# An adaLN transformer block on one core: the MLP's slices and output units in turn, in groups of four and two, with clamp, products and the second norm moved off VectorE

## The chip, the core and the metric

The kernel runs on one core of a Trainium2 chip. A core has five engines with queues of their own: TensorE (PE; its weight loads are listed as PEld), VectorE (DVE), ScalarE (ACT), GpSimd (POOL) and SyncE (SP), which issues all of this kernel's DMAs. Each engine runs its queue in order and waits on semaphores of the others. The metric is the device time of one execution in microseconds (us), as the median of several runs. Chances below speak of faster and slower by over 0.5%, which is about what a measurement of this kernel can tell from no change.

## The reference

```python
x = A_x                                        # 1 x 2048 x 512, fp32
mod = (silu(c) @ w_mod).reshape(1, 6, 1, 512)
sa, ca, ga, sb, cb, gb = (mod[:, i] for i in range(6))
h = layernorm(x) * (1 + ca) + sa
x = x + ga * attention(h, A_wqkv, A_wo)        # 32 heads of 16, softmax over all 2048 keys
h = layernorm(x) * (1 + cb) + sb
x = x + gb * (mish(h @ B_w1 + B_b1) @ B_w2)    # 512 -> 1792 -> 512, mish(h) = h * tanh(softplus(h))
```

With e = exp(h) and p = e(e + 2), tanh(softplus(h)) is p / (p + 2). The kernel caps the exponent's argument at HCAP = 10 and takes the reciprocal as exp(-ln(p + 2)), refined by one Newton step. Matrix products are made of three, from high and low parts of their factors (hi x hi, hi x lo, lo x hi).

## The kernel before

**Steps.** Attention is a loop of 512 steps (T). A step t handles, for one group of four heads and one block of 512 queries, one chunk of 128 keys: four score products (L507), four exponentials on ACT (L513) and the four products with the values for step t-2 (L531). It also makes four products for the row maxima of a group 20 steps (PRO) ahead (L470), which DVE reduces (L472), up to step 491. Sixteen steps finish a head group; eight groups (128 steps) finish a query block. The row maxima of a group are put together every 16 steps (L481 to L490).

**Slots.** Score and maximum products use 64 of the array's 128 rows, and two products in different halves run side by side. MLP and projection products are split into two halves of 64 rows (`mm_half`, L128), the first half of a unit's share in an even step, the second in the odd step after it. A *unit* is a list of matmuls that add up into one bank. `next_part` (L989) takes a unit of at most 8 matmuls whole into a pair of steps, and a longer one in two halves. Part of the maxima change over to the half that has fewer products (L1067). The six banks `ring` are shared by scores and maxima, `bk` with tags ms and acc is for units and values.

**Units beside attention.** For each of the first three query blocks (`block`, L746), once its attention is ready, 4 units project (`wo_unit`, 12 matmuls, L767), then 14 up slices (`up_unit`, 12 matmuls and the Mish, L808) and down units (`down_unit`, L825) for each group of slices and each 128 rows i. A unit is taken from a queue in order, once its ready time has come. Groups are of 5, 5 and 4 slices in blocks 0 and 1, so 15, 15 and 12 matmuls; in block 2 of 4, 4, 3 and 3, of which the last two (eight units) are held for the tail. The fourth block's projection and MLP are done in the tail, when attention has ended.

**Half steps.** `at(h, f)` runs f at half step h; a step t has half steps 2t and 2t+1 (at its middle). What a unit's end sets off is placed by h: for an up slice the bias at once, the clamp one half step later, then its exponential, the product p on DVE and h times p on POOL, the logarithm, and with the reciprocal's exponential all of POOL's rest (L719 to L735).

**Buffers.** Tags of the pool `mp` give a number of buffers: hb 3, ee 2, rr 2, a_h and a_l 7 each (NA), w2 7 (it also takes the projection's weights), w1 2; yd shares rr's two. A new use of a buffer waits for the last reader of the old one.

**Lines.** Second norm: `layernorm` (L100; statistics on DVE, L104 and L105, three POOL operations L106, L107, L109). Splits into high and low part: L95 and L98 on POOL. Attention's output is divided and split on POOL at L574, L95 and L98 after its denominators have gone to memory and back (L567, L569). Output units are copied by ACT (L835) and added on POOL (L836).

Of the kernel before, what the change touches and what calls it, by code (L numbers as in the profile page):

```python
# [18 lines left out]
def adaln_block(ctx: ExitStack, tc: tile.TileContext, x, wqkv, wo, w1, b1, w2, c, w_mod, out):  # L19
    nc = tc.nc  # L20
# [640 lines left out]
    def load_wo(k):  # L661
        return load_split("w2", NA, woscr[k])

# [3 lines left out]
    def load_w2(f):  # L667
        return load_split("w2", NA, w2scr[f])

    def w1v(w, v, k):  # L670
        return w[:, v, k * P:(k + 1) * P]

    def load_y(qb, i):
        y = mst["p"].tile([P, D], F32, tag=f"y{i}", name="y", bufs=1)
# [18 lines left out]
    def mish(f, acc, tail):  # L693

        mp = mst["p"]
        hb = mp.tile([P, TB], F32, tag="hb", name="hb", bufs=3)
        ee = mp.tile([P, TB], F32, tag="ee", name="ee", bufs=2)
        rr = mp.tile([P, TB], F32, tag="rr", name="rr", bufs=2)
        qq = mp.tile([P, TB], F32, tag="qq", name="qq", bufs=1)
        a_h = mp.tile([P, TB], F32R, tag="a_h", name="a_h", bufs=NA)  # L700
        a_l = mp.tile([P, TB], F32R, tag="a_l", name="a_l", bufs=NA)

        def s1(late=False):
            if late:
                nc.vector.tensor_scalar_add(hb, acc, b1c[:, f:f + 1])
            else:
                nc.scalar.activation(hb, acc, AF.Identity, bias=b1c[:, f:f + 1])

        def s2():
            nc.scalar.activation(ee, hb, AF.Relu, bias=hcap, scale=-1.0)  # L710

        def s2b():
            nc.scalar.activation(ee, ee, AF.Exp, bias=hcap, scale=-1.0)  # L713

        def s3():
            nc.vector.scalar_tensor_tensor(ee, ee, 2.0, ee, op0=ALU.add, op1=ALU.mult)  # L716
            (nc.vector if tail else nc.gpsimd).tensor_mul(hb, hb, ee)  # L717

        def s4():  # L719
            nc.scalar.activation(rr, ee, AF.Ln, bias=two)  # L720

        def s5():
            nc.scalar.activation(rr, rr, AF.Exp, scale=-1.0)  # L723
            if tail:
                nc.vector.scalar_tensor_tensor(qq, ee, 2.0, rr, op0=ALU.add, op1=ALU.mult)
                nc.vector.scalar_tensor_tensor(rr, qq, 2.0, rr, op0=ALU.subtract, op1=ALU.mult)
                nc.vector.scalar_tensor_tensor(hb, hb, -1.0, rr, op0=ALU.mult, op1=ALU.mult)
            else:
                nc.gpsimd.tensor_scalar(ee, ee, 1.0, 2.0, op0=ALU.mult, op1=ALU.add)
                nc.gpsimd.tensor_mul(qq, ee, rr)  # L730
                nc.gpsimd.tensor_scalar(qq, qq, -1.0, 2.0, op0=ALU.mult, op1=ALU.add)
                nc.gpsimd.tensor_mul(rr, rr, qq)  # L732
                nc.gpsimd.tensor_mul(hb, hb, rr)  # L733
            hi_copy("v" if tail and f > FT - 4 else "p", a_h, hb)
            lo_sub("v" if tail and f > FT - 4 else "p", a_l, hb, a_h)  # L735

        return (a_h, a_l), (s1, s2, s2b, s3, s4, s5)
# [5 lines left out]
    first_loads_of, early_loads_of = {}, {}  # L743
    NA = 7

    def block(qb, t0):  # L746

        xn, y, act, w1s, w2s, wos, done, hx = {}, {}, {}, {}, {}, {}, {}, []
        cuts = (0, 5, 10, 14) if qb < NB - 2 else (0, 4, 8, 11, 14)
        groups = [list(range(a, b)) for a, b in zip(cuts, cuts[1:])]  # L750
# [6 lines left out]
        def early_loads(h):  # L757
            load(h, wos, load_wo, range(DK - 1))

        def first_loads(h):  # L760
            load(h + 1, wos, load_wo, range(len(wos), DK))
            load(h + 2, y, lambda i: load_y(qb, i), range(4))
            load(h + 9, w1s, load_w1, range(2))
            load(h + 10, w2s, load_w2, range(NA - DK))
            done["w"] = h + 3

        def wo_unit(i, tag):  # L767
# [7 lines left out]
            def fin(h):  # L775
                nc.vector.tensor_add(y[i], acc, y[i])

                def norm():
                    xn[i], a = norm_y(y[i])
                    at(h + 3, a)  # L780
# [3 lines left out]
                if i == 3:  # L784
                    load(h + 1, w2s, load_w2, range(NA - DK, NA))
# [465 lines left out]
```

## Time and profile before

| what | us |
|---|---|
| median of three runs (1737.65 to 1745.74) | 1743.94 |
| the profiled execution | 1742.38 |
| its span on the core | 1740.6 |
| PE busy | 1699.3 |
| DVE busy | 1464.0 |
| ACT busy | 1341.4 |
| POOL busy | 752.8 |

The span is the time from the first to the last instruction on the core; a run's own time is some 2 us longer. A group's row reads: line, engine, operation, out <- in with shapes, count | busy time in all, mean of one in ns | idle time of the engine just before, and what ended it. A timeline's row reads: start, length, engine, line, operation, count, and in brackets the idle time before it and its releaser. A window's row gives for each engine the busy time and in brackets the number of instructions, then the granted clock and the share of the DMA engines. Busy time of PE counts overlapping matmuls once, and includes time in which one drains.

### The profile page before, as it was taken

The page shows a single profiled execution, that of the slowest core. Times are in us where ns is not written, and L with a number is a line of the kernel's source. Part 1 is how long each engine was busy: PE and PEld are TensorE (multiplying, and loading weights), DVE is VectorE, ACT ScalarE, POOL GpSimd, SP SyncE. Part 2 cuts the span into 40 slices and gives each one's busy share as a digit, 9 for nine tenths or more (in the row PEclk, how much of TensorE's full clock was granted, in tenths as well). Part 3 has the DMA queues.
Part 4 walks back from the last instruction along what each step waited for, and adds up shares of the span by engine and source line. Part 5 has one row for each costly group of instructions (what it writes and reads, how often), then busy time and mean ns, then how long its engine had stood idle before and what let it go on. Part 6 is the DMA issues. An engine that isn't in the chain of part 4 may idle for free.

```text
span 1740.6 us, 32834 instructions
## 1 busy us (share of the span) xinstructions
PE 1699.3 (98%) x12230; PEld 942.2 (54%) x12230; DVE 1464.0 (84%) x2464; ACT 1341.4 (77%) x2565; POOL 752.8 (43%) x740
## 2 busy tenths in 40 slices
PE   7999999999999999999999999999999999999999
PEld 5755655545435555555455455555455455554687
DVE  6988888878889898888989998888989999891477
ACT  6257777777777898897877898797877899898474
POOL 5245224656303274362312275273312277172852
PEclk9999999999999999999999999999999999999999
DMA  7777457777763342433345543442435334422361
GB/s 255 183 227 213 120 157 234 210 230 221 233 174 94 95 115 79 130 98 80 91 121 132 134 108 90 123 114 56 114 88 158 110 103 102 127 80 79 147 230 61
DMA packets 113991, 240.01 MB, mean 138 GB/s; under 512 B 24048, under 2 KB 49648, under 8 KB 107784
## 3 DMA queue, kind: packets, MB, share of 16 engines
q1 hardware_dynamic: 113832, 237.92, 48.2%
q8 instruction: 96, 1.57, 0.4%
q14 instruction: 63, 0.52, 0.1%
HBM read 179.95 MB, written 51.44 MB: 133 GB/s over the span
## 4 chain that ended last, share of the span: by engine, by line
PE 80%; DMA 6%; DVE 4%; ACT 4%; POOL 3%; SPq 2%; issue 1%; POOLq 0%; ACTq 0%; DVEq 0%
PE bk L531 26%; PE ring L470 19%; PE ring L507 18%; PE bk L132 11%; ACT pr L513 2%; DVE mx L472 2%; PE ring L126 2%; DMA qscr<-ql 1%; PE ring L966 1%; DMA w2scr<-hl 1%; PE bk L126 1%; DMA kscr<-ql 1%; DMA xt<-in_A_x 1%; DMA hl<-in_B_w 1%; DMA wm<-in_w_mod 0%
## 5 line engine op out<-in xcount | busy, mean ns | idle before, releaser
L472 DVE TENSOR_REDUCE mx<-ring 128x1 f32<-128x512 f32 x2048 | 1273.7, 682 | 167.8 <-PE ring L470 132.6
L513 ACT ACTIVATE pr<-ring 128x512 f32<-128x512 f32 x2048 | 1080.2, 604 | 265.4 <-PE bk L132 144.1
L470 PE MATMUL ring<-ka,qa 64*128 64x512 f32 x2048 | 840.3, 427 | 1.1 <-DVE mx L472 0.2
L507 PE MATMUL ring<-qa,ka 64*128 64x512 f32 x2048 | 736.4, 400 | 11.7 <-ACT pr L513 9.9
L470 PEld LDWEIGHTS ring<-ka,qa 64*128 64x128 f32 x2048 | 364.2, 184 | 396.7 <-DVE mx L472 324.1
L531 PE MATMUL bk<-pr,vg 128*32 128x512 f32 x4096 | 546.1, 605 | 0.0
L507 PEld LDWEIGHTS ring<-qa,ka 64*128 64x128 f32 x2048 | 371.7, 184 | 120.0 <-ACT pr L513 63.4
L132 PE MATMUL bk<-h,w 64*128 64x512 f32 x996 | 275.6, 409 | 1.3 <-ACT pr L513 1.2
L132 PEld LDWEIGHTS bk<-h,w 64*128 64x128 f32 x996 | 171.1, 184 | 17.6 <-ACT pr L513 7.7
L132 PE MATMUL bk<-w,a_h 64*128 64x512 f32 x576 | 167.2, 414 | 0.2
L531 PEld LDWEIGHTS bk<-pr,vg 128*32 128x32 f32 x4096 | 80.7, 108 | 138.4 <-issue 133.1
L836 POOL TENSOR_TENSOR y<-yd,y 128x512 f32<-128x512 f32 x40 | 52.0, 1305 | 212.2 <-ACT yd L835 191.7
L717 POOL TENSOR_TENSOR hb<-hb,ee 128x512 f32<-128x512 f32 x42 | 54.0, 1287 | 176.1 <-DVE ee L716 176.1
L132 PEld LDWEIGHTS bk<-w,a_h 64*128 64x128 f32 x576 | 96.5, 184 | 12.2 <-ACT pr L513 6.6
L730 POOL TENSOR_TENSOR qq<-ee,rr 128x512 f32<-128x512 f32 x42 | 54.4, 1295 | 75.2 <-ACT rr L723 72.7
L132 PE MATMUL bk<-w,o_hl 64*128 64x512 f32 x288 | 80.0, 409 | 1.3 <-POOL o_hl L95 0.7
L132 PE MATMUL bk<-w,a_l 64*128 64x512 f32 x288 | 77.0, 391 | 0.0
L98 POOL TENSOR_TENSOR a_l<-hb,a_h 128x512 fp32r<-128x512 f32 x53 | 72.4, 1366 | 4.4
L132 PE MATMUL bk<-h_h,wl 64*128 64x512 f32 x168 | 57.1, 420 | 0.0
L716 DVE SCALAR_TENSOR_TENSOR ee<-ee 128x512 f32<-128x512 f32 x56 | 39.9, 712 | 19.3 <-ACT ee L713 19.3
L733 POOL TENSOR_TENSOR hb<-hb,rr 128x512 f32<-128x512 f32 x42 | 54.5, 1297 | 3.3
L732 POOL TENSOR_TENSOR rr<-rr,qq 128x512 f32<-128x512 f32 x42 | 54.2, 1290 | 3.5
(187 smaller groups left out, 1724.8 us busy)
## 6 DMA issues: line engine op xcount, KB each, us to landing
ka<-kscr SPq DMA_DIRECT2D x124, 384.0 KB
w<-w2scr SPq DMA_DIRECT2D x56, 512.0 KB
w<-w1scr SPq DMA_DIRECT2D x46, 512.0 KB
vg<-vscr SPq DMA_DIRECT2D x32, 552.0 KB
qa<-qscr SPq DMA_DIRECT2D x124, 100.0 KB
kscr<-qh SPq DMA_DIRECT2D x16, 512.0 KB
qscr<-qh SPq DMA_DIRECT2D x32, 256.0 KB
hl<-in_B_w SPq DMA_DIRECT2D x28, 256.0 KB
```

What stands on the lines that cost most here:

```text
L98: (nc.gpsimd if eng == "p" else nc.vector).tensor_sub(lo, src, hi.bitcast(F32))
L126: nc.tensor.matmul(acc, l, r, start=start, stop=stop)
L132: i = nc.tensor.matmul(acc, l[64 * g:64 * g + 64], r[64 * g:64 * g + 64], start=start, stop=stop)
L470: nc.tensor.matmul(pm, qt[64 * s:64 * s + 64, qs * P:(qs + 1) * P], kt[64 * s:64 * s + 64, kb * TB:(kb + 1) * TB], start=True, stop=True)
L472: nc.vector.tensor_reduce(out=mxs[n][:, s, 4 * j + qs, kb:kb + 1], in_=pm, op=ALU.max, axis=AX.X)
L507: nc.tensor.matmul(p_, kt[64 * s:64 * s + 64, kc * P:(kc + 1) * P], qt[64 * s:64 * s + 64, :], start=True, stop=True)
L513: e = nc.scalar.activation(pr, p_, AF.Exp, scale=SCALE)
L531: nc.tensor.matmul(accs[n][32 * h:32 * h + 32, :], vgs[n][:, o:o + 32], pts.pop((t, h)), start=(kc == 0), stop=(kc == 15))
L717: (nc.vector if tail else nc.gpsimd).tensor_mul(hb, hb, ee)
L730: nc.gpsimd.tensor_mul(qq, ee, rr)
L732: nc.gpsimd.tensor_mul(rr, rr, qq)
L733: nc.gpsimd.tensor_mul(hb, hb, rr)
```

## The change

Per block, groups are now of 4, 4, 4 and 2 slices for all blocks. The queue is written out by `all_blocks`: the last group's down unit 0 of the block before, the four projections, the other three of those down units, six up slices, then eight times a down unit and an up slice, then the third group's down units. Of block 2, eight units (groups 2 and 3) are held for the tail as before, 12 and 6 matmuls long. Down units go slice by slice (high and low parts of one slice together). The Mish outside the tail has its clamp and all products on POOL, and its stages are spread over 18 half steps. The second norm's sum and sum of squares come from ACT. yd has one buffer of its own, a_h and a_l eight, w2 six. The residual rows y rotate over seven tiles, two of them the gates' after their use.

```diff
     def load_wo(k):
-        return load_split("w2", NA, woscr[k])
+        return load_split("w2", NW, woscr[k])
...
     def norm_y(y):
-        xn = mst["p"].tile([P, D], F32, tag="a_h", name="xn2", bufs=NA)
-        return xn, layernorm(mst["p"], y, xn, "p")
+        mp = mst["p"]
+        xn = mp.tile([P, D], F32, tag="hb", name="xn2", bufs=3)
+        ss = mp.tile([P, 4], F32, tag="ln_s", name="ln_s", bufs=4)
+
+        def mean():
+            nc.scalar.activation(xn, y, AF.Identity, accum_out=ss[:, 0:1])
+            nc.gpsimd.tensor_scalar(ss[:, 1:2], ss[:, 0:1], -1.0 / D, 0.0, op0=ALU.mult, op1=ALU.add)
+
+        def spread():
+            nc.scalar.activation(xn, y, AF.Square, bias=ss[:, 1:2], accum_out=ss[:, 2:3])
+            nc.gpsimd.tensor_scalar(ss[:, 2:3], ss[:, 2:3], 1.0 / D, EPS, op0=ALU.mult, op1=ALU.add)
+            nc.gpsimd.tensor_tensor(ss[:, 3:4], ss[:, 2:3], nhalf, op=ALU.pow)
+            nc.gpsimd.tensor_scalar(xn, y, ss[:, 1:2], ss[:, 3:4], op0=ALU.add, op1=ALU.mult)
...
-        def s2():
-            nc.scalar.activation(ee, hb, AF.Relu, bias=hcap, scale=-1.0)
...
+        def clamp():
             if tail:
+                nc.scalar.activation(buf("ee", 2), b["hb"], AF.Relu, bias=hcap, scale=-1.0)
+            else:
+                nc.gpsimd.tensor_scalar(buf("ee", 2), b["hb"], HCAP, 0.0, op0=ALU.min, op1=ALU.add)
...
-        def s3():
-            nc.vector.scalar_tensor_tensor(ee, ee, 2.0, ee, op0=ALU.add, op1=ALU.mult)
-            (nc.vector if tail else nc.gpsimd).tensor_mul(hb, hb, ee)
...
+            else:
+                nc.gpsimd.tensor_scalar(rr, ee, 1.0, 2.0, op0=ALU.mult, op1=ALU.add)
+                nc.gpsimd.tensor_mul(ee, ee, rr)
+                nc.gpsimd.tensor_mul(hb, hb, ee)
...
-    NA = 7
+    NA, NW = 8, 6
+    GROUPS = [list(range(a, min(a + 4, FT))) for a in range(0, FT, 4)]
...
             def fin(h):
-                nc.vector.tensor_add(y[i], acc, y[i])
-
-                def norm():
-                    xn[i], a = norm_y(y[i])
-                    at(h + 3, a)
-
-                at(h + 1, norm)
-                done["xn", i] = h + 3
+                yd = mst["p"].tile([P, D], F32, tag="yd", name="yd", bufs=1)
+                nc.scalar.copy(yd, acc)
+                nc.gpsimd.tensor_add(y[i], yd, y[i])
+
+                def mean():
+                    xn[i], first, then = norm_y(y[i])
+                    first()
+                    at(h + 5, then)
+
+                at(h + 3, mean)
+                done["xn", i] = h + 7
...
             def fin(h):
-                stages[0](idle(h))
-                for i, s in zip((1, 2, 3, 4, 6), stages[1:]):
+                bias(idle(h))
+                for i, s in zip((1, 3, 4, 9, 13, 13, 16, 18), stages):
                     at(h + i, s)
-                done["a", f] = h + 6
...
+                done["a", f] = h + 20
...
-            mm3(acc, [act[f][0][:, s] for f in fs], [act[f][1][:, s] for f in fs],
-                [w2s[f][:, 0, :] for f in fs], [w2s[f][:, 1, :] for f in fs])
+            seq = [(act[f][v][:, s], w2s[f][:, r, :]) for f in fs for v, r in ((0, 0), (0, 1), (1, 0))]
...
-                yd = mst["p"].tile([P, D], F32, tag="rr", name="yd", bufs=2)
+                yd = mst["p"].tile([P, D], F32, tag="yd", name="yd", bufs=1)
...
+    def all_blocks():
+
+        for qb in range(NB - 1):
+            blocks.append(block(qb, 32 * G * (qb + 1) + 14))
+        for qb, b in enumerate(blocks):
+            wo, up, down = (b["units"][k] for k in ("wo", "up", "down"))
+            before = blocks[qb - 1]["units"]["down"] if qb else lambda gi, i: None
+            before(3, 0)
+            for i in range(4):
+                wo(i)
+            for i in range(1, 4):
+                before(3, i)
+            for f in range(6):
+                up(f)
+            for j in range(8):
+                down(j // 4, j % 4)
+                up(6 + j)
+            for i in range(4 if qb < NB - 2 else 0):
+                down(2, i)
+        at(2 * T - 30, tail_loads)
```

POOL's queue in a run of up slices. Before, one slice after another (L717 is h times p, L729 to L733 the quotient, L95 and L98 the split):

```order
L717 TENSOR_TENSOR hb<-hb,ee 128x512
L729 TENSOR_SCALAR ee<-ee 128x512
L730 TENSOR_TENSOR qq<-ee,rr 128x512
L731 TENSOR_SCALAR qq<-qq 128x512
L732 TENSOR_TENSOR rr<-rr,qq 128x512
L733 TENSOR_TENSOR hb<-hb,rr 128x512
L95 TENSOR_SCALAR a_h<-hb 128x512
L98 TENSOR_TENSOR a_l<-hb,a_h 128x512
```

Now (L732 is the clamp, L746 to L748 the products, L763 to L767 the quotient; line numbers of the changed file):

```order
L732 TENSOR_SCALAR ee<-hb 128x512
L95 TENSOR_SCALAR a_h<-hb 128x512
L98 TENSOR_TENSOR a_l<-hb,a_h 128x512
L574 TENSOR_TENSOR od<-od,rb 128x512
L95 TENSOR_SCALAR o_hl<-od 128x512
L98 TENSOR_TENSOR o_hl<-od,o_hl 128x512
L746 TENSOR_SCALAR rr<-ee 128x512
L747 TENSOR_TENSOR ee<-ee,rr 128x512
L748 TENSOR_TENSOR hb<-hb,ee 128x512
L763 TENSOR_SCALAR ee<-ee 128x512
L764 TENSOR_TENSOR ee<-ee,rr 128x512
L765 TENSOR_SCALAR ee<-ee 128x512
```

Eight operations of one slice have become eleven, of three slices in turn: a clamp, the split of the slice two before, the products, and the quotient of the slice before. L574 with its split, which belongs to attention, stands between them once in each run.

ACT's queue at the end of an up slice, with the scores' exponentials (L513) between. Before (L707 bias, L710 clamp, L713 exponential):

```order
L707 ACTIVATE hb<-bk,b1c 128x512
L513 ACTIVATE pr_0_1182<-ring 128x512
L513 ACTIVATE pr_2_1151<-ring 128x512
L710 ACTIVATE ee<-hb,hcap 128x512
L513 ACTIVATE pr_2_1159<-ring 128x512
L513 ACTIVATE pr_3_1152<-ring 128x512
L513 ACTIVATE pr_3_1160<-ring 128x512
L713 ACTIVATE ee<-ee,hcap 128x512
```

Now (L726 bias, L751 the logarithm of the slice before, L738 the exponential):

```order
L726 ACTIVATE hb<-bk,b1c 128x512
L513 ACTIVATE pr_1_1183<-ring 128x512
L513 ACTIVATE pr_2_1151<-ring 128x512
L751 ACTIVATE rr<-ee,two 128x512
L513 ACTIVATE pr_2_1159<-ring 128x512
L513 ACTIVATE pr_3_1152<-ring 128x512
L513 ACTIVATE pr_3_1160<-ring 128x512
L513 ACTIVATE pr_2_1177<-ring 128x512
L738 ACTIVATE ee<-ee 128x512
```

L738 waits for POOL's clamp; L713 waited for ACT's own.

SP's queue where block 1's projection begins (woscr: projection weights; rscr, rb: the denominators out and back; ka, qa: keys and queries). Before:

```order
L839 DMA out<-y 128x512
L567 DMA rscr<-rc 128x16
L293 DMA qa_107<-qscr 50x512 x2
L302 DMA ka_105<-kscr 48x2048 x2
L569 DMA rb<-rscr 64x1x512
L839 DMA out<-y 128x512
L457 DMA vg<-vscr 128x1104
L839 DMA out<-y 128x512
L658 DMA w_9817<-woscr 128x1024
```

Now:

```order
L658 DMA w_9581<-woscr 128x1024
L658 DMA w_9609<-woscr 128x1024
L567 DMA rscr<-rc 128x16
L658 DMA w_9643<-woscr 128x1024
L293 DMA qa_107<-qscr 50x512 x2
L302 DMA ka_105<-kscr 48x2048 x2
L569 DMA rb<-rscr 64x1x512
L658 DMA w_9676<-woscr 128x1024
L888 DMA out<-y_5264 128x512
```

Three of the four projection weights were loaded earlier before, and the fourth after rb; now all four stand around the denominators' round trip.

More of the change, by code (lines that the diff above doesn't have):

```diff
@@ L695, in mish, with buf @@
         mp = mst["p"]
[L696 to L703, printed above, removed]
+        b, a = {}, []
+        def buf(tag, bufs):
+            if tag not in b:
+                b[tag] = mp.tile([P, TB], F32, tag=tag, name=tag, bufs=bufs)
+            return b[tag]
@@ L829, in down_unit @@
             s = slice(i * P, (i + 1) * P)
[L830 to L831 removed]
+            seq = [(act[f][v][:, s], w2s[f][:, r, :]) for f in fs for v, r in ((0, 0), (0, 1), (1, 0))]
+            for j, (l, r) in enumerate(seq):
+                mm(acc, l, r, j == 0, j == len(seq) - 1)
+            then = blocks[qb + 1] if qb + 1 < len(blocks) else None
+            if gi == 2 and i == 3 and not held and then:
+                load(cur["h"] + 5, then["wo"], load_wo, range(2))
```

169 lines of the change are left out of this document (98 added, 71 removed).

## The prediction

> **What bounds the kernel now.** I read the page first, then the groups by line, then windows cut at step borders, then timelines of one up slice, one block border and the tail.
>
> ```profile
> span 1740.6 us, 32834 instructions
> PE 1699.3 (98%) x12230; PEld 942.2 (54%) x12230; DVE 1464.0 (84%) x2464; ACT 1341.4 (77%) x2565; POOL 752.8 (43%) x740
> L472 DVE TENSOR_REDUCE mx<-ring 128x1 f32<-128x512 f32 x2048 | 1273.7, 682 | 167.8 <-PE ring L470 132.6 <-PE bk L132 33.1 <-PE ring L507 0.9
> ```
>
> PE is always busy and POOL idles for more than half of the span. A busy PE is not yet the limit, so I price steps. Each step ends with eight records of L531, so a window's count over eight gives its steps (columns: width, PE busy with its count, PEld busy with its count, clock, DMA).
>
> ```profile
> 508.01:1567.22 1059.21, 379.28 (x2848) 56.01 (x2848) 1.00 0.40 106
> 1567.22:1621.42 54.20, 21.31 (x160) 3.15 (x160) 1.00 0.31 112
> 909.19:958.12 48.93, 17.05 (x128) 2.51 (x128) 1.00 0.50 135
> 975.81:1058.31 82.50, 29.83 (x224) 4.40 (x224) 1.00 0.37 95
> 1058.31:1107.93 49.62, 17.05 (x128) 2.52 (x128) 1.00 0.32 69
> 875.00:903.41 28.41, 10.65 (x80) 1.57 (x80) 1.00 0.41 106
> 458.40:477.60 19.20, 7.46 (x56) 1.10 (x56) 1.00 0.79 227
> 1575.20:1593.84 18.64, 7.46 (x56) 1.10 (x56) 1.00 0.04 9
> ```
>
> The first two rows are the stretch in which MLP work runs beside attention: 376 steps (136 to 511), 1113.4 us, and the change lies in it. By kind of step: output projection 48.93/16 = 3.06 us; seven up slices in a row 82.50/28 = 2.95; down units of five slices (15 matmuls, as eight and seven) 49.62/16 = 3.10; down units of four slices, six matmuls a step, 28.41/10 = 2.84; no MLP work 19.20/7 = 2.74; six matmuls after the row maxima have ended 18.64/7 = 2.66. The full clock (1.00) is granted throughout. So a step with six MLP matmuls needs 2.84 when nothing disturbs it, only 0.10 more than an empty one, and up slices, long down units and the projection cost more than that.
>
> Why an up slice costs more is seen on DVE:
>
> ```profile
> 1028.78 0.68 DVE L716 SCALAR_TENSOR_TENSOR ee<-ee 128x512 f32<-128x512 f32 x1
> 1029.38 3.74 DVE L472 TENSOR_REDUCE mx<-ring 128x1 f32<-128x512 f32 x6
> 1036.34 2.48 DVE L472 TENSOR_REDUCE mx<-ring 128x1 f32<-128x512 f32 x4 [0.37 <-PE ring L470]
> ...
> L470 PEld LDWEIGHTS ring<-ka,qa 64*128 64x128 f32 x2048 | 364.2, 184 | 396.7 <-DVE mx L472 324.1
> ```
>
> Four maxima end after 2.48, so they start 0.60 apart and fill 2.4 of 2.84 us; with L716 between them, itself 0.60 to the next, five take 3.0, more than the step. Then PE's weight load of L470 waits for a bank of the ring.
>
> **Edit 1, the order of units.** Per block: 4 projections of 12 matmuls, 14 up slices of 12, 12 down units of 12, 4 of 6. At six matmuls a step that is 16 + 56 + 48 + 8 = 128 steps, just what a block of attention lasts. The program's order has six MLP matmuls in every step from 136 to 501, but for 152 to 157; from 502 to 511 there are none. So 360 steps carry MLP work, against 342 and a spill of half a slice behind step 511 before. The long down units (3.10) go.
>
> **Edit 2, DVE freed.** L716, the projection's sum and its norm statistics leave DVE until the tail; in a step it keeps four maxima, 2.4 us. Nothing then stands between the ring and PE but ACT, with four exponentials (2.06) and one more operation (0.7):
>
> ```profile
> 1030.87 2.06 ACT L513 ACTIVATE pr<-ring 128x512 f32<-128x512 f32 x4 [0.17 <-PE ring L507]
> 926.60:930.12 3.52, 3.46 (x29) 1.95 (x27) 3.30 (x7) 2.60 (x6) 0.86 (x1) 1.00 1.04 298
> 860.60:863.66 3.06, 3.06 (x25) 1.49 (x23) 2.95 (x7) 2.07 (x6) 0.00 (x0) 1.00 0.02 5
> ```
>
> The two windows are a step with four transposes (3.52, so +0.68; 12 of them stay) and one with a head group's row maxima (3.06, +0.22; 23 stay).
>
> The floor of the stretch: 350 x 2.84 = 994.0; 10 x 2.66 = 26.6; six empty steps x 2.74 = 16.4; ten empty steps without maxima, between the four exponentials' 2.06 and 2.66, taken as 2.3 = 23; transposes 8.2; row maxima 5.1. Sum 1073, so 40 us less than 1113.4 if nothing new waits.
>
> **Edit 3, what is loaded onto GpSimd.** These are the prices:
>
> ```profile
> L98 POOL TENSOR_TENSOR a_l<-hb,a_h 128x512 fp32r<-128x512 f32 x53 | 72.4, 1366 | 4.4
> L731 POOL TENSOR_SCALAR qq<-qq 128x512 f32<-128x512 f32 x42 | 26.4, 629 | 3.7
> L109 POOL TENSOR_SCALAR xn<-y,ln_mv,ln_rs 128x512 f32<-128x512 f32 x12 | 25.0, 2082 | 1.3
> 1033.60 1.29 POOL L730 TENSOR_TENSOR qq<-ee,rr 128x512 f32<-128x512 f32 x1 [2.06 <-ACT rr L723]
> 1034.98 0.63 POOL L731 TENSOR_SCALAR qq<-qq 128x512 f32<-128x512 f32 x1
> 1035.69 1.30 POOL L732 TENSOR_TENSOR rr<-rr,qq 128x512 f32<-128x512 f32 x1
> ```
>
> Start to start, a two-input operation takes 1.38 and one with constants 0.71. A slice now has six of the first (product 2, quotient 3, split 1) and five of the second (clamp, product, quotient 2, split): 8.28 + 3.55 = 11.8 us, where it had 5 x 1.38 + 3 x 0.71 = 9.0. Alternating with a down unit (8 steps, 22.7 us, plus an addition of 1.4) this fits. In the run of six up slices a slice lasts 4 x 2.84 = 11.4, so the queue falls behind by 0.4 each time, and at the fourth the attention output's three operations (L574, L95, L98: 3.5 us) stand in the same queue. The exponential behind a clamp is issued three half steps (4.3 us) after the bias. Following the queue by these prices, the first four clamps come in time; the fifth ends 3.7 us late, and the sixth another 0.5. ACT stands at that exponential with the next scores queued behind it, and PE goes on until the six banks are full; about 1.5 us of it is hidden, some six products. Cost: 2.7 us a run, 8 for three. Bounds: 0 if the cover is longer, (6 x 0.4 + 3.5) x 3 = 18 if there is none. The clamp itself, minimum then addition of constants, has no row: between 0.63 (L731, two constants) and 2.08 (L109, two per-partition scalars). I take 0.63, the same form with another operation.
>
> [...]
>
> The removed L716 also cost POOL something:
>
> ```profile
> 1016.37 1.61 DVE L716 SCALAR_TENSOR_TENSOR ee<-ee 128x512 f32<-128x512 f32 x1
> 1016.15 1.29 POOL L574 TENSOR_TENSOR od<-od,rb 128x512 f32<-128x512 f32 x1
> ```
>
> It took 1.61 instead of 0.68 beside a POOL operation. [...]
>
> **Edit 4, block borders.** The last two slices' down units now stand between and behind the projections, so blocks 1 and 2 start their projection at steps 264 and 392 without a pause. Its last quarter needs attention output that POOL splits only then:
>
> ```profile
> 889.82 0.61 SPq L569 DMA_DIRECT2D rb<-rscr  x1
> 897.77 1.27 POOL L574 TENSOR_TENSOR od<-od,rb 128x512 f32<-128x512 f32 x1 [3.36 <-DMA rb<-rscr]
> 899.84 1.29 POOL L98 TENSOR_TENSOR o_hl<-od,o_hl 128x512 fp32r<-128x512 f32 x1
> 516.53 0.49 PE L132 MATMUL bk<-w,o_hl 64*128 64x512 f32 x1 [0.66 <-POOL o_hl L95]
> 517.88 0.50 PE L132 MATMUL bk<-w,o_hl 64*128 64x512 f32 x1 [0.62 <-POOL o_hl L98]
> ```
>
> In block 0 PE already waits for it, about 2 us with the maxima that stop too. For block 1 step 266, whose half unit needs it, would start eight steps of 2.84 after 875.00 (the end of step 257), at 897.7 of the old time; the low part is due near 899 and was ready at 901.1: again 2.1. Sum 2 + 2 x 2.1 = 6. On SP two projection weights are now ahead of the denominators' store and a third ahead of their reload rb; if that delays rb (7.9 us from issue to use above), it adds to it. Bounds 2 and 16.
>
> **Edit 5, the second norm by ACT.** Sum and squares are two ACT operations of 0.7 to 0.8 each in steps with room. Behind the squares stand three POOL operations:
>
> ```profile
> 525.71 0.19 POOL L106 TENSOR_SCALAR ln_rs<-ln_mv 128x1 f32<-128x1 f32 x1 [7.88 <-DVE ln_mv L105]
> 526.65 2.09 POOL L109 TENSOR_SCALAR xn<-y,ln_mv,ln_rs 128x512 f32<-128x512 f32 x1
> ```
>
> From the first to the end of the last (526.65 + 2.09 - 525.71) 3.0 us, after the squares. ACT comes to a mid-step operation 1.26 us after the step's first product:
>
> ```profile
> 1035.80 0.50 PE L470 MATMUL ring<-ka,qa 64*128 64x512 f32 x1
> 1037.06 0.71 ACT L710 ACTIVATE ee<-hb,hcap 128x512 f32<-128x512 f32 x1
> 1037.73 0.64 PE L531 MATMUL bk<-pr,vg 128*32 128x512 f32 x4
> ```
>
> So squares (1.26 in, 0.75 long) and chain end 5.0 after that first product, or 5.1 with a handover. The transposes stand at the end of the next step's products, 2.84 + 1.93 - 0.1 = 4.7. So 0.4 x 12 = 5; bounds 0 and 20 (an addition of 1.3 ahead in the queue each time). ACT now waits for GpSimd at every clamp, and the one yd buffer makes each copy wait for the addition before it, where there were two: 2, bounds 0 and 8.
>
> **Tail.** It loses the spilled half slice on PE (1.7 us) and the activation chain that lay beside it. Against that:
>
> ```profile
> 1655.37 1.07 ACT L835 COPY yd<-ring 128x512 f32<-128x512 f32 x2
> 1656.68 5.48 POOL L836 TENSOR_TENSOR y<-yd,y 128x512 f32<-128x512 f32 x4
> 1661.13 0.69 ACT L707 ACTIVATE hb<-bk,b1c 128x512 f32<-128x512 f32 x1 [0.84 <-PE bk L126]
> ```
>
> With one yd buffer five copies and additions run one after the other, some 2.1 us each, before the tail's first bias on ACT: 10.5 against 5.8 here, 4.7 later, after a start some 3 to 5 earlier. I take 0, bounds -3 and +5.
>
> **Sum.** New waits 8 + 6 + 5 + 2 = 21. Stretch 1073 + 21 = 1094, 19 less than 1113.4. Span 1740.6 - 19 = 1721.6. The profiled execution itself took 1742.38, 1.8 around its span, and 1.56 under the median of the runs, 1743.94; so 1723.4 for such a run and 1725 at the median. I say 1724.
>
> **Rivals.** (a) Nothing new waits that matters: clamp and transposes in time, the border waits as before, tail 3 better. 1073 + 6 leaves 34 + 3, so 1707. For it: POOL at 43%. Against: 11.8 in 11.4. Chance 0.17. (b) Block borders eat it: weights and rb late by 5 us more at two borders, and transposes late by 0.5 more: 10 + 6, so 1740. For it: 1.5 MB of weights beside keys and rb. Against: DMA shares of 0.3 to 0.5. Chance 0.11. (c) GpSimd becomes the bound, and the kernel slower: if the clamp costs L109's 2.08, a slice takes 13.3 in 11.4. Followed as above, a run of six loses 9 instead of 2.7 (+19); between down units the clamp, behind a quotient of 5.6, ends at 4.4 us where 4.1 is due (24 x 0.3 = 7); and split slices reach their down units 2 late in each block (6). 1724 + 32 = 1756. It decides from a clamp of about 2.1 us. For it: no row of this form. Against: L731. Chance 0.14. That the change doesn't do what it says is excluded by the order. My forecast has 0.58.
>
> **Range and chances.** Its own bounds, 1713 to 1736, come from half of the new waits' swing either way; the range, with (a) and most of (b), is 1706 to 1746, and leaves (c) out. Faster by over 0.5% (under 1735; less is no difference that this measurement tells) has 0.17 and most of 0.58: 0.70. Within: (b) and the rest, 0.16. Slower: 0.14.
>
> **What would show it.** Right: windows of up slices at 2.85 to 2.90 a step except the end of each run of six; no L472 wait of PE beyond its own; POOL over 90% there. ACT idle before the clamp's exponential, released by POOL, near the fifth slice, 3 us a block; L132 waiting on o_hl at steps 266 and 394. Wrong: a clamp far from 0.63; idle steps inside blocks; up slices still near 2.95, which would mean that DVE was not their limit; a tail longer by over 5 us.

## The result, and the profile after

The changed kernel takes 1760.97 us in the median of five runs (1757.53 to 1761.91); the kernel before took 1743.94 (five runs, 1737.65 to 1747.15). The ratio is 1.0099, with a 95% interval of 1.0075 to 1.0123: slower by 1%, where 1724 was predicted. The profiled execution took 1760.91.

The changed kernel's page, its head and three of its groups:

```profile
span 1759.1 us, 32844 instructions
PE 1703.3 (97%) x12236; PEld 973.7 (55%) x12236; DVE 1423.9 (81%) x2384; ACT 1345.7 (77%) x2593; POOL 921.1 (52%) x898
L732 POOL TENSOR_SCALAR ee<-hb 128x512 f32<-128x512 f32 x42 | 80.7, 1921 | 48.2 <-ACT hb L726 45.2
L132 PE MATMUL bk<-h,w 64*128 64x512 f32 x1008 | 283.0, 413 | 15.2 <-ACT pr L513 15.2
L132 PE MATMUL bk<-w,o_hl 64*128 64x512 f32 x288 | 85.1, 426 | 7.4 <-POOL o_hl L95 6.5
```

VectorE lost 40 us of work and GpSimd gained 168, as the edits said. New are two idle times of PE (15.2 and 7.4 us), at the up slices' products and at the projection's, and the clamp L732 takes 1.92 us, not 0.63. The same two groups before:

```profile
L132 PE MATMUL bk<-h,w 64*128 64x512 f32 x996 | 275.6, 409 | 1.3 <-ACT pr L513 1.2
L132 PE MATMUL bk<-w,o_hl 64*128 64x512 f32 x288 | 80.0, 409 | 1.3 <-POOL o_hl L95 0.7 <-POOL o_hl L98 0.6
```

Windows of L531 again cut the stretch (eight records are a step; columns as in the prediction). The rows are the stretch, the first run of six up slices, the first alternate phase, and the second block's border:

```profile
506.54:1639.18 1132.64, 405.68 (x3008) 59.41 (x3008) 0.98 0.39 105
577.25:660.67 83.42, 28.56 (x209) 4.14 (x209) 0.96 0.39 99
660.67:892.08 231.41, 85.23 (x640) 12.59 (x641) 1.00 0.41 106
892.08:966.95 74.87, 24.31 (x176) 3.50 (x176) 0.95 0.30 76
```

The stretch (steps 136 to 511, up to the last of attention) takes 1132.6 where it took 1113.4. That is the whole loss: what lies ahead of it is 1.5 shorter (506.5 against 508.0), the tail 0.8 longer (119.9 against 119.1). In the rows of the run of six and of the border the granted clock is below 1.00.

The run of six ends like this. First GpSimd, then ScalarE, then PE, from the timeline:

```profile
614.93 1.92 POOL L732 TENSOR_SCALAR ee<-hb 128x512 f32<-128x512 f32 x1
627.75 1.92 POOL L732 TENSOR_SCALAR ee<-hb 128x512 f32<-128x512 f32 x1
631.68 1.30 POOL L574 TENSOR_TENSOR od<-od,rb 128x512 f32<-128x512 f32 x1
643.86 1.92 POOL L732 TENSOR_SCALAR ee<-hb 128x512 f32<-128x512 f32 x1
...
645.81 0.63 ACT L738 ACTIVATE ee<-ee 128x512 f32<-128x512 f32 x1 [4.44 <-POOL ee L732]
...
647.47 0.79 PE L132 MATMUL bk<-h,w 64*128 64x512 f32 x1 [3.99 <-ACT pr L513]
```

GpSimd works without a pause. From clamp to clamp it needs 12.8 us (627.75 - 614.93), and 16.1 with the attention output's three operations from L574 on, while PE sends a slice every 11.4. ScalarE stands 4.44 us at the exponential L738, the scores' exponentials are queued behind it, and PE stops for 3.99. PE's matmul then takes 0.79 where it took 0.40. Windows over all engines show why (columns after the length: PE, PEld, DVE, ACT, POOL busy, granted clock, DMA share, GB/s):

```profile
643.20:646.60 3.40, 0.27 (x1) 0.00 (x0) 0.69 (x1) 0.79 (x2) 3.15 (x4) 1.00 0.79 186
646.63:653.46 6.83, 6.00 (x25) 3.12 (x27) 2.10 (x4) 3.96 (x8) 6.50 (x7) 0.50 0.23 52
653.46:657.70 4.24, 4.24 (x34) 2.73 (x32) 3.79 (x7) 3.73 (x7) 3.99 (x4) 1.00 0.34 124
```

After 3.40 us in which PE was busy for 0.27, its clock is granted at 0.50 for 6.83 us. So step 180 takes 8.76 and step 181 4.08 in place of 2.84 each: 7.2 lost, 4.0 of it the stop and 3.2 the half clock. Steps 308 and 436 (8.74 and 8.72) are like it: stops of 3.97 and 3.94, and 0.50 for 6.83 us each time.

The border of the second block, from the timeline: SyncE's issues, GpSimd, and PE's waits in step 266. Then two windows of L531, steps 266 and 267:

```profile
888.16 0.38 SPq L658 DMA_DIRECT2D w<-woscr  x1
888.60 0.73 SPq L293 DMA_DIRECT2D qa<-qscr  x2
889.37 0.78 SPq L302 DMA_DIRECT2D ka<-kscr  x2
890.25 0.60 SPq L569 DMA_DIRECT2D rb<-rscr  x1
...
900.54 1.26 POOL L574 TENSOR_TENSOR od<-od,rb 128x512 f32<-128x512 f32 x1 [6.11 <-DMA vg<-vscr]
...
902.57 0.76 PE L132 MATMUL bk<-w,o_hl 64*128 64x512 f32 x1 [2.63 <-POOL o_hl L95]
...
897.75:905.07 7.32, 1.06 (x8) 0.15 (x8) 0.83 0.63 194
905.07:909.90 4.83, 1.94 (x9) 0.21 (x9) 0.55 0.00 0
```

L574 follows the issue of rb by 10.3 us, where it was 7.9 before (897.77 against 889.82). The bracket names the values' load vg; but L574 reads od and rb alone, so rb's landing on the same queue is the likelier releaser (run 5 tests it; in run 4's trace the bracket of this wait names rb). PE waits 2.63, and again the clock falls: 0.50 for 6.83 us from 902.63 on. The two steps take 12.15 in place of 2.84 each, 6.5 lost.

### The profile page after: what moved, and what is told of

The parts are those of the page before. It is cut to its first block, busy times and chain, and to the rows that moved or that the text cites. A ratio compares the mean times of both kernels' runs of the same rounds, so it can differ in the third digit from the quotient of the medians.

```text
span 1759.1 us, 32844 instructions
## 1 busy us (share of the span) xinstructions
PE 1703.3 (97%) x12236; PEld 973.7 (55%) x12236; DVE 1423.9 (81%) x2384; ACT 1345.7 (77%) x2593; POOL 921.1 (52%) x898
## 4 chain that ended last, share of the span: by engine, by line
PE 77%; DMA 10%; POOL 4%; ACT 3%; DVE 3%; SPq 2%; issue 1%; POOLq 0%; ACTq 0%; DVEq 0%
PE bk L531 25%; PE ring L470 18%; PE ring L507 17%; PE bk L132 11%; PE ring L126 2%; DMA qscr<-ql 2%; ACT pr L513 2%; PE ring L1047 1%; DVE mx L472 1%; DMA w2scr<-hl 1%; DMA kscr<-ql 1%; PE bk L126 1%; DMA vg<-vscr 1%; DMA hl<-in_B_w 1%; DMA ka<-kscr 1%
## 5 line engine op out<-in xcount | busy, mean ns | idle before, releaser
L513 ACT ACTIVATE pr<-ring 128x512 f32<-128x512 f32 x2048 | 1100.9, 606 | 263.4 <-PE bk L132 148.1
L507 PE MATMUL ring<-qa,ka 64*128 64x512 f32 x2048 | 725.9, 401 | 7.2 <-ACT pr L513 6.7
L531 PE MATMUL bk<-pr,vg 128*32 128x512 f32 x4096 | 551.8, 611 | 0.0
L132 PE MATMUL bk<-h,w 64*128 64x512 f32 x1008 | 283.0, 413 | 15.2 <-ACT pr L513 15.2
L132 PE MATMUL bk<-w,a_h 64*128 64x512 f32 x576 | 193.8, 416 | 0.8 <-ACT pr L513 0.5
L531 PEld LDWEIGHTS bk<-pr,vg 128*32 128x32 f32 x4096 | 81.5, 108 | 140.4 <-issue 132.9
L132 PE MATMUL bk<-w,a_l 64*128 64x512 f32 x288 | 113.2, 393 | 0.0
L764 POOL TENSOR_TENSOR ee<-ee,rr 128x512 f32<-128x512 f32 x42 | 53.8, 1280 | 108.5 <-ACT rr L754 107.2
L732 POOL TENSOR_SCALAR ee<-hb 128x512 f32<-128x512 f32 x42 | 80.7, 1921 | 48.2 <-ACT hb L726 45.2
L98 POOL TENSOR_TENSOR a_l<-hb,a_h 128x512 fp32r<-128x512 f32 x53 | 71.7, 1354 | 4.4
L132 PEld LDWEIGHTS bk<-w,o_hl 64*128 64x128 f32 x288 | 51.6, 193 | 12.6 <-POOL o_hl L95 7.8
L574 POOL TENSOR_TENSOR od<-od,rb 128x512 f32<-128x512 f32 (+1 forms) x16 | 20.6, 1289 | 71.3 <-DMA vg<-vscr 57.9
L747 POOL TENSOR_TENSOR ee<-ee,rr 128x512 f32<-128x512 f32 x42 | 54.1, 1289 | 3.5
## 6 DMA issues: line engine op xcount, KB each, us to landing
w<-w2scr SPq DMA_DIRECT2D x56, 512.0 KB
w<-w1scr SPq DMA_DIRECT2D x46, 512.0 KB
kscr<-qh SPq DMA_DIRECT2D x16, 512.0 KB
```

What stands on the lines that cost most here:

```text
L98: (nc.gpsimd if eng == "p" else nc.vector).tensor_sub(lo, src, hi.bitcast(F32))
L132: i = nc.tensor.matmul(acc, l[64 * g:64 * g + 64], r[64 * g:64 * g + 64], start=start, stop=stop)
L507: nc.tensor.matmul(p_, kt[64 * s:64 * s + 64, kc * P:(kc + 1) * P], qt[64 * s:64 * s + 64, :], start=True, stop=True)
L513: e = nc.scalar.activation(pr, p_, AF.Exp, scale=SCALE)
L531: nc.tensor.matmul(accs[n][32 * h:32 * h + 32, :], vgs[n][:, o:o + 32], pts.pop((t, h)), start=(kc == 0), stop=(kc == 15))
L732: nc.gpsimd.tensor_scalar(buf("ee", 2), b["hb"], HCAP, 0.0, op0=ALU.min, op1=ALU.add)
```

## The experiments

Three theories came out of these views. Theory 1: the clamp's price overloads GpSimd in the runs of six. Theory 2: at the borders rb lands late. Theory 3 is for the rest, since the alternate phase takes 2.89 a step at full clock without any stop: ScalarE's operations lie in the way of PE. The rivals stand in the expectations.

The part of the program ahead of step 136 ended anywhere from 504.1 to 512.0 us in the profiled executions, whatever the edit. So beside each run's median stands its stretch, measured as above. The changed kernel is 1760.97 and 1132.6; the kernel before, run again beside each group, was 1743.4, 1743.0 and 1744.3.

**Run 1: the clamp's operation alone.**

```diff
-nc.gpsimd.tensor_scalar(buf("ee", 2), b["hb"], HCAP, 0.0, op0=ALU.min, op1=ALU.add)
+nc.gpsimd.tensor_scalar(buf("ee", 2), b["hb"], 0.25, 0.0, op0=ALU.mult, op1=ALU.add)
```

> The changed kernel (1760.97) with GpSimd's clamp computed as a product with 0.25 in place of the minimum with 10: the limit is left out and the exponential gets a quarter of its argument, all else stays. Theory 1 (the price of the minimum, 1.92 us, overloads GpSimd in each run of six up slices, and ScalarE and TensorE stop behind it): the operation takes about 0.63, a slice on GpSimd shrinks from 12.8 to 11.5 us, the stops of 8.7 us at steps 180, 308 and 436 go, and so does the half granted clock behind them: 1761 - 24 = 1737, between 1732 and 1742. Rival A (the run of six is overloaded in any case, by the products and the attention output's three operations; a stop of any size brings the half clock with it): at most a third of it goes, 1753 or more. Rival B (the block borders are the loss): no change beyond 5 us, 1756 or more.

Measured: 1741.39 (ratio to before 0.999, 0.9977 to 1.0004), stretch 1111.1. The group of the clamp, the first run of six, and ScalarE near its end:

```profile
L732 POOL TENSOR_SCALAR ee<-hb 128x512 f32<-128x512 f32 x42 | 26.2, 623 | 45.2 <-ACT hb L726 45.2
573.17:649.69 76.52, 27.71 (x209) 4.10 (x209) 1.00 0.43 108
...
637.54 0.63 ACT L738 ACTIVATE ee<-ee 128x512 f32<-128x512 f32 x1 [1.27 <-POOL ee L732]
```

Same place, same operands, same bytes: 0.62 with a product, 1.92 with a minimum. The run falls from 83.4 to 76.5 at full clock, three runs by 20 in all, which is as much as the whole difference of the two kernels. Of the stand of 4.44 at L738 1.27 is left. Theory 1 holds; A and B don't. But 1741 is still not 1724: two more causes are left.

**Run 2: the clamp on VectorE.** The same line with `nc.vector.tensor_scalar` and the minimum.

> The changed kernel with the clamp on VectorE (minimum, then addition, 42 of them outside the tail), all else stays. Theory 1: GpSimd is relieved by 2.0 us a slice, the stops at the ends of the runs of six go as in the run with the product (-24), and VectorE, with 2.4 of 2.84 us a step taken by the maxima, takes one more operation every four steps: at 0.4 us it fits, at 0.7 it costs up to 0.2 a slice (+8). So 1737 to 1745. Rival C (any operation more on VectorE between the maxima costs PE its whole length, as the up slices of the kernel before suggest): 42 x 0.6 = 25 comes back, 1757 to 1762.

Measured: 1749.06 (1.0037, 1.0025 to 1.005), stretch 1121.8. The run of six is 77.1, so the stop of step 180 and its half clock are gone; the alternate phase is 234.1 instead of 231.4, some 7 in all three phases: worse than theory 1 had it (1745 at most) and far from C's 25. Run 6 shows what these are.

**Run 3: a later projection at the borders.**

```diff
-            before(3, 0)
+            for i in range(2):
+                before(3, i)
             for i in range(4):
                 wo(i)
-            for i in range(1, 4):
+            for i in range(2, 4):
                 before(3, i)
```

> The changed kernel with two down units instead of one ahead of the next block's projection, so that it starts two steps (5.7 us) later at the second and third block; the clamp stays as it is. Theory 2 (at the border the attention output of the last head group is late by 2.6 us because its denominators' reload lands late, and the stop brings the half clock): the excess of 6.5 us at steps 266 and 394 goes, the first block's 3.7 stays, and two idle steps a border behind the projection move work to the end of the stretch at almost no cost: 1761 - 12 = 1749, between 1746 and 1753. Rival D (the output or the transposes only become late elsewhere): 1757 to 1763.

Measured: 1753.53 (1.0067, 1.0046 to 1.0089), stretch 1124.0, 8.6 less where 12 was expected, and the time lies just above theory 2's range. Windows of L531: steps 262 to 285, and a piece of the last steps, which have no MLP work:

```profile
886.54:961.02 74.48, 25.57 (x193) 3.77 (x193) 1.00 0.35 87
1625.90:1632.70 6.80, 3.89 (x20) 0.43 (x20) 0.50 0.46 175
```

The first row has two steps more than the 74.87 above: from 264 on it is 68.8, 6.1 less, at full clock. Both borders gain that, as theory 2 says. But the work moved to the end cost 7.0 there: the last ten steps take 27.4 instead of 20.4. ScalarE stands 1.77 at L738 for the last clamp, and at the half clock behind it step 509 takes 4.65 where it took 1.97. The other 3.4 of the 8.6 were gained in parts that the edit doesn't touch (the first projection 1.8, the second run of six 1.9), so they are put down to chance.

**Run 4: the product back on VectorE.**

```diff
-                nc.gpsimd.tensor_scalar(rr, ee, 1.0, 2.0, op0=ALU.mult, op1=ALU.add)
-                nc.gpsimd.tensor_mul(ee, ee, rr)
+                nc.vector.scalar_tensor_tensor(ee, ee, 2.0, ee, op0=ALU.add, op1=ALU.mult)
```

> The changed kernel with one part undone: the product (e+2)e is again one VectorE operation with two inputs, so GpSimd loses 2.1 us a slice (a product with constants and a product of two), while the clamp stays on GpSimd at 1.92. Theory 1 (it is the length of GpSimd's queue that stops ScalarE, not the clamp's form): the stops at the ends of the runs go (-24), and VectorE's fifth operation costs an up slice what it cost before, 2.95 against 2.84 a step, 0.44 a slice, 42 x 0.44 = 18: 1755, between 1748 and 1760. Rival E (the queue is not it: the clamp comes late by its place in the program): the stops stay, 1775 or more. Rival F (VectorE was not what made the up slices long): 1737.

Measured: 1745.37 (1.0008, 0.9996 to 1.002), stretch 1117.2. Its first run of six and first alternate phase:

```profile
578.01:655.85 77.84, 27.70 (x208) 4.10 (x209) 1.00 0.43 106
655.85:887.33 231.48, 85.23 (x641) 12.58 (x641) 1.00 0.41 106
```

With the clamp still at 1.92 the long stops are gone: it is the length of GpSimd's queue that counts. And 231.48 against 231.41 says that VectorE's fifth operation costs the alternate phase nothing. A run of six takes 1.3 more than in run 1, at two steps: step 176 takes 3.79 (2.85 in run 1), where the product on VectorE takes 1.63 instead of 0.68 beside L574 and PE waits 0.65 for the maxima behind it, and step 172 takes 3.31 (2.87). The time misses theory 1's range from below: VectorE costs 4 us, not the 18 I gave it, so rival F is nearer; its 1737 counts 24 for the stops, of which run 1 shows 20.

**Run 5: the reload ahead of the keys** (with run 4's edit).

```diff
-        at(2 * t1 + (13 if hurry else 17),
+        at(2 * t1 + (12 if hurry else 17),
```

> The run with the product on VectorE (1745.37), with the denominators' reload rb of a block's last head group issued one half step sooner, so that on SP's queue it stands ahead of the next queries and keys (two loads each) and behind one projection weight. Theory 2 (at a border the last head group's attention output is late because its reload lands late, and each stop brings a half granted clock): the waits of L132 for o_hl go at steps 138, 266 and 394, with the slow steps behind them: 2 to 4 at the first and 6 each at the others, 1745 - 15 = 1730, between 1727 and 1735. Rival D (the reload is late by the weights alone, or the wait only moves to the weights or the transposes): 1740 or more. Rival G (the keys, now later by the reload's wait, stop the scores of the next group): over 1745.

Measured: 1732.78 (0.9943, 0.9928 to 0.9958), stretch 1102.8, 14.4 less than run 4. SyncE's issues at the second border, GpSimd's and PE's waits there:

```profile
879.63 0.38 SPq L658 DMA_DIRECT2D w<-woscr  x1
880.63 0.60 SPq L569 DMA_DIRECT2D rb<-rscr  x1
881.29 0.84 SPq L293 DMA_DIRECT2D qa<-qscr  x2
882.17 0.78 SPq L302 DMA_DIRECT2D ka<-kscr  x2
...
885.83 1.30 POOL L574 TENSOR_TENSOR od<-od,rb 128x512 f32<-128x512 f32 x1
...
892.26 0.47 PE L132 MATMUL bk<-w,o_hl 64*128 64x512 f32 x1 [0.86 <-DMA w<-woscr]
```

L574 follows the issue of rb by 5.2 us, without a wait, where it followed by 10.0 in run 4 (895.56 against 885.51). The issue itself came only 1.1 sooner behind the store (1.4 instead of 2.5), so the rest is its place ahead of the keys. PE no longer waits for the attention output. 0.86 is left for the fourth projection weight; the clock stays at 1.00 over the whole stretch. The reload behind the keys was the cause of the late output, and this kernel beats both.

**Run 6: clamp and product on VectorE** (run 5 with run 2's edit).

> The run before this one with the clamp on VectorE too, so GpSimd loses another 2.0 us a slice (some 8.8 of 11.4 us left in the runs of six) and VectorE has two operations a slice. Theory 1: what is left of the stops in the runs of six (0.5, 0.9 and 1.3 us at three steps of each run, 8 in all) goes, and VectorE's second operation fits into the steps: 8 less than the run before it, at best 1722. Rival C (VectorE's queue: a clamp that waits for its buffer holds the maxima behind it, as in the run with the clamp alone there, whose alternate steps took 2.93 instead of 2.89): 2 to 8 more than the run before it.

Measured: 1737.70 (0.9965, 0.9951 to 0.9978), stretch 1108.2, 5.4 more than run 5. The runs of six gain 1.1 each, but the alternate phase is 234.7. From the timeline, a clamp of VectorE beside a GpSimd operation, and the clamps' durations (minimum, median, maximum in ns) by line:

```profile
672.90 1.29 POOL L98 TENSOR_TENSOR a_l<-hb,a_h 128x512 fp32r<-128x512 f32 x1
673.01 1.46 DVE L732 TENSOR_SCALAR ee<-hb 128x512 f32<-128x512 f32 x1
...
L732 DVE TENSOR_SCALAR ee<-hb x42: 417/419/1557, 590.2 to 1598.0; 128x512 f32<-128x512 f32 x42
```

The clamp needs 0.42, but one that starts 0.11 after L98 ends 0.28 after it. Rival C holds in its mildest form: not every operation costs its length, but in four of the eight slices of an alternate phase the clamp falls beside L98, takes 1.46 or more, and the step behind it takes 3.56 instead of 2.84. The clamp has one input; L716, which took 1.61 beside L574 in the kernel before, has two.

**Run 7: two operations fewer on ScalarE** (run 1 without L738 and L751 outside the tail).

> The run with GpSimd's clamp as a product (1741.39), with two of ScalarE's five operations of a slice left out outside the tail: the exponential behind the clamp and the logarithm. Theory 3 (the alternating steps take 2.89 instead of the 2.84 of a quiet step because an operation of ScalarE between two steps' exponentials holds the next step's first MLP product by 0.05 to 0.12): the alternate phase falls from 2.894 to 2.86 a step or less, 84 operations less at 0.07 are 6: 1735, between 1732 and 1738. Rival H (the length comes from VectorE or from PE's own weight loads): the phase stays at 2.89, 1740 to 1742.

Measured: 1729.03 (0.9923, 0.9908 to 0.9939), stretch 1098.8, 12.3 less than run 1. ScalarE and PE in steps 202 and 203 of the changed kernel, step 203's window there, and the same step of this run:

```profile
714.95 0.71 ACT L751 ACTIVATE rr<-ee,two 128x512 f32<-128x512 f32 x1
715.56 1.56 ACT L513 ACTIVATE pr<-ring 128x512 f32<-128x512 f32 x3
716.55 0.50 PE L470 MATMUL ring<-ka,qa 64*128 64x512 f32 x1
716.69 0.50 PE L132 MATMUL bk<-h,w 64*128 64x512 f32 x1
715.55:718.51 2.96, 1.06 (x8) 0.16 (x8) 1.00 0.00 0
...
707.39:710.24 2.85, 1.06 (x8) 0.15 (x8) 1.00 0.69 215
```

L751 holds the exponentials behind it; so the step's first MLP product starts 0.14 after the first maximum's product instead of beside it, and the step is longer by about that. Without it the step takes 2.85. The first alternate phase falls from 231.4 to 229.8, a run of six from 76.5 to 74.9, the last twenty steps by 2: in all twice the 6 expected, so the time misses the range from below, though a step of the alternate phase falls to 2.87 only, not to 2.86 or less. Theory 3 holds against H: the steps behind L738 and L751 reach 2.84, and those with the bias, which stays, remain at 2.94 or above. In the changed kernel's alternate phases the steps that have no such operation in them or in the step before take 2.83.

**Runs 8 and 9: the clamp on ScalarE**, in the changed kernel and in run 5's.

```diff
-            if tail:
-                nc.scalar.activation(buf("ee", 2), b["hb"], AF.Relu, bias=hcap, scale=-1.0)
-            else:
-                nc.gpsimd.tensor_scalar(buf("ee", 2), b["hb"], HCAP, 0.0, op0=ALU.min, op1=ALU.add)
+            nc.scalar.activation(buf("ee", 2), b["hb"], AF.Relu, bias=hcap, scale=-1.0)
```

> The changed kernel (1760.97) with one part undone: the clamp is ScalarE's rectifier again, as in the kernel before, and the exponential behind it takes the limit back off; the products stay on GpSimd. Theory 1 (moving the clamp to GpSimd made the stops in the runs of six): they go, as in the run with the product in its place (-24), and ScalarE's sixth operation of a slice costs 0.05 to 0.12 of a step by theory 3 (42 x 0.07 = +3): 1740, between 1736 and 1745. Rival A (GpSimd overloaded in any case): 1753 or more. Rival I (ScalarE has no room for a sixth operation, and that is why it was taken off): each costs its own 0.6, 42 x 0.6 = +25, so 1760.

> The run with the product on VectorE and the reload ahead of the keys (1732.78), with the clamp on ScalarE as in the run before this one. Theories 1 and 3: the 1.2 us at step 180 and its like go (-4), 42 operations on ScalarE cost 3, so 1732, between 1728 and 1736. Rival I: 25 more for ScalarE, 1754. Rival J (the products that are left on GpSimd come earlier now and take VectorE's product and the quotient's out of each other's way): down to 1726.

Measured: 1750.88 (1.0038, 1.0025 to 1.0051), stretch 1122.6; and 1739.33 (0.9975, 0.9964 to 0.9987), stretch 1109.3. Both miss theory 1's range from above. The changed kernel with it, first run of six, and ScalarE in one step of it:

```profile
576.79:655.67 78.88, 27.70 (x208) 4.09 (x208) 1.00 0.42 104
602.06 0.71 ACT L745 ACTIVATE rr<-ee,two 128x512 f32<-128x512 f32 x1
602.67 0.71 ACT L729 ACTIVATE ee<-hb,hcap 128x512 f32<-128x512 f32 x1
603.28 2.26 ACT L513 ACTIVATE pr<-ring 128x512 f32<-128x512 f32 x4
```

The long stops are gone (78.9 at full clock, from 83.4), so the clamp on GpSimd made them, on top of the products there (run 4). But in a run the clamp now falls into the half step of the last slice's logarithm, and a step with two such operations takes 3.47 to 3.49 (steps 167, 171, 175 and 183): 0.6 there, not 0.07. That is rival I's price, where two meet; in the alternate phase, where they don't, a slice costs 0.1.

**Run 10: edit 5 undone** (run 5 with the projection's sum, L776 of the kernel before, and the norm's statistics on VectorE).

> The run with the product on VectorE and the reload ahead of the keys (1732.78), with edit 5 undone: the projection's sum is VectorE's addition from the bank again, and the second norm's statistics are VectorE's, with GpSimd's normalisation by subtraction (about 2.1 us instead of 0.77). Theory 3 (what an edit puts on ScalarE in a step costs the next step): the steps behind the transposes fall from 3.25 to 2.84, 12 x 0.4 = 5, and the steps with sums and squares (3.05, 2.98) stay, since VectorE's operations cost as much there: 1728, between 1725 and 1731. Rival K (VectorE has no room beside four maxima, each of its operations costs 0.6): 12 x (3 x 0.6 - 0.4 - 0.35) = +13, 1746.

Measured: 1731.82 (0.9924, 0.9900 to 0.9948), stretch 1101.4: the same as run 5 within what can be told, and 0.8 above the range expected. The steps behind the transposes fall from 3.25 to 2.84, as theory 3 says, and the steps with VectorE's sum and statistics rise to 3.30 and 3.18 at each block's first. Edit 5 is worth nothing that can be told either way.

## Why the prediction was wrong

The stretch in parts, in us. The forecast is the prediction's prices put on each part; the steps of the kernel before hold other units there, so its column is only for size.

| part (steps) | before | forecast | changed | run 1 | run 5 |
|---|---|---|---|---|---|
| first projection, transposes (136 to 151) | 51.5 | 52.0 | 52.9 | 51.2 | 49.2 |
| before the first up slice (152 to 157) | 17.9 | 16.6 | 17.8 | 17.8 | 17.8 |
| three runs of six (78 steps) | 231.1 | 230.4 | 249.5 | 229.6 | 233.5 |
| alternate phases (212 steps) | 627.6 | 605.0 | 613.6 | 613.6 | 613.6 |
| two borders (44 steps) | 131.1 | 138.6 | 149.9 | 149.8 | 139.6 |
| 492 to 501 | 26.6 | 26.6 | 28.6 | 28.6 | 28.6 |
| 502 to 511 | 27.6 | 23.0 | 20.4 | 20.4 | 20.4 |
| ScalarE's waits, anywhere | | 2.0 | | | |
| sum | 1113.4 | 1094.2 | 1132.6 | 1111.1 | 1102.8 |

**Edit 3, the step that decided it.** "The clamp itself ... I take 0.63, the same form with another operation." It was 1.92. The chain (clamp late, ScalarE stands at the fifth slice's exponential, PE stops) was right. With a clamp of 0.62 the sum of a run holds too: run 1 needs 76.5 a run, the forecast 76.8. That is in part luck: only 1.3 of the 2.7 is the stop (step 180 takes 4.13), the rest ScalarE's small holds of theory 3. Rival (c) had the mechanism, at 9 a run for a clamp of about 2.1; measured are 9.1 (83.2 a run, less 76.8, and the 2.7 that these hold), of which some 3 are the half clock that (c) doesn't have. Its other two prices, for the alternate phase and the late split slices, did not come: the phase is the same in runs 1 and 4. So that its 1756 lies near 1761 is luck as well: the borders and ScalarE's holds took the place of those 13. The row that priced the clamp was chosen for its form, and the other row of the same form, L109, was put down to its operands. In the changed kernel that normalisation adds instead of subtracting, with the same kind of operands, and takes 0.77; in run 10, which brings the subtraction back, it takes 2.08 again:

```profile
L698 POOL TENSOR_SCALAR xn<-y,ln_s 128x512 f32<-128x512 f32 x10 | 7.7, 772 | 1.1
...
L109 POOL TENSOR_SCALAR xn<-y,ln_mv,ln_rs 128x512 f32<-128x512 f32 x10 | 20.8, 2084 | 0.9
```

So L109's 2.08 was the price of its arithmetic, and its 2.08 lay nearer to the minimum's 1.92 than L731's 0.63.

**Edit 4 was mis-sized, by what no term held.** The wait at a later border was forecast at 2.1 and was 2.8 (2.63 and 0.16). Around it the half clock, which the prediction leaves out although its own rows show a granted clock, took most of the other 3.7 (12.15 - 2 x 2.84 - 2.8) at each of the two. In the first block the waits of the kernel before (0.66 and 0.62) cost 2.0 and left the clock at 1.00; here they were 0.84 and 0.62, the clock was 0.50 for 3.41 us behind them, and steps 138 and 139 took 5.30 and 4.14. The three borders cost 3.8 and 2 x 6.5, 16.8 where 6 was forecast and 16 was the bound. The delay of rb that the bounds allowed for was real (10.3 against 7.9), and run 5 shows its cause.

**The floor's 350 x 2.84 was too low.** "Nothing then stands between the ring and PE but ACT, with four exponentials (2.06) and one more operation (0.7)": the sum, 2.76, fits into 2.84, but not wherever the operation falls. Steps with or behind one take up to 2.96, and the alternate phases are 8.6 over the forecast. Run 7 takes 4.4 of that away with two of the operations; the rest stands at the steps with or behind the others, which no run removed. The reading behind edit 2 was wrong too, by the prediction's own sign: with four maxima alone on VectorE an up slice in run 1's runs of six still takes 2.94 a step (76.5/26), or 2.89 without the stop of step 180, and run 4 shows that VectorE's fifth operation does not lengthen the alternate phase. That the phase gained 14 against the kernel before is left to the new order and to ScalarE's operations lying further apart; no run tells these two apart.

**Right:** the tail (0 forecast, 0.8 measured), the last ten steps (cheaper still), the transposes' 5 (12 x 0.41 by the steps behind them, though ScalarE's copy of the projection's sum ahead of L840 makes it, not a late norm, so that its size came by luck).

**The range.** Half of the way from the new waits, 21, to their upper bounds, 62, is 20, so by those bounds the upper end was 1744 and not 1736; 1761 lies beyond it all the same.

From the forecast to the measured stretch: runs +19.1, borders +11.3, alternate phases +8.6, first projection +0.9, 152 to 157 and 492 to 501 +3.2, the last ten -2.6, ScalarE's own term -2.0: 38.5, where 1132.6 - 1094.2 is 38.4. What makes steps 152 to 157 and 492 to 501 take 3.2 more than forecast stays open.

## What to carry to other kernels

Price an operation by a row with the same arithmetic, not only the same form; where the only rows of the form lie a factor of three apart, find what divides them before choosing one, since a queue at 11.8 of 11.4 us turns that choice into the sign of the result. Work that is moved onto an engine in the path must be placed, not only counted: one more operation on ScalarE cost 0.1 or 0.6 by the half step it fell into. And a small load that others wait for goes ahead of the large ones on its queue: half a step sooner was worth 12.6 us here (run 5 against run 4), the half clock included.

## What the hardware showed that was not expected

- A stop of PE cost more than its length. After the five stops of 2.63 to 3.99 us in the changed kernel's stretch the granted clock was 0.50 for 6.83 us each, and about twice the stop was lost (7.2 for 4.0; 6.5 for 2.8).
- It need not be one stop. At step 138 PE waited 0.84 and then 0.62 in the changed kernel, and the clock was 0.50 for the 3.41 us from 516.9 on. In the kernel before the two waits were 0.66 and 0.62, and it stayed at 1.00. What makes the difference is left open.
- GpSimd's price of an operation with one input went by the arithmetic, on 128x512: with constants 0.62 for product and addition (run 1), 1.92 for minimum and addition (the changed kernel); with a scalar per partition 0.77 for addition and product (the changed kernel), 2.08 for subtraction and product (the kernel before and run 10).
- VectorE's one-input minimum, 0.42 at the median, took 1.46 beside a two-input operation of GpSimd (run 6).
